# First expert matrix: transfers with 32 or 128 partitions outermost in place of 4

## The chip, the cores and the metric

The kernel runs on one NeuronCore of a Trainium2 chip. The metric is device time in microseconds (us), from start to end of one execution; less is better. Engines are called by the profile's names: PE (TensorE matmul), PEld (its weight loads), ACT (ScalarE), DVE (VectorE), POOL (GpSimd), SP (SyncE, whose queue issues most DMA transfers).

## The reference

Two layers follow each other.

1. A spectral layer on x (8 batches, 2496 positions, 256 channels, float32): a real FFT along the positions, a complex 256x256 matrix with bias per frequency, a soft threshold, and the inverse FFT.
2. A mixture of experts on its 19968 tokens: a 256x8 gate picks one of 8 experts per token (argmax), and the token gets `gate * (relu(x @ w1[e]) @ w2[e])` with w1[e] of 256x1024 and w2[e] of 1024x256, all float32.

```python
for e in range(E):
    xe = x[expert_idx == e]
    h = np.maximum(xe @ w1[e], 0.0)
    out[mask] = gate_w[mask, None] * (h @ w2[e])
```

## The kernel before

**The spectral part** (about the first 640 us) computes the FFTs as matrix products, gates each token, and writes every token's row with an indirect DMA into a DRAM buffer, `xs_dram`, in which the rows of one expert stand together. It is not touched.

**The expert part** works on tiles of 256 tokens. All tokens of a tile have the same expert, and tiles stand in the order of the experts. There are 85 tiles at most; tiles 0 to 81 always run, the last 3 sit behind branches (L902 to L909). A small table, built on the chip (`table`, L619), gives for each tile its expert (word 0), whether it needs its weights loaded (word 1: 1 for the first tile of a table and for a tile whose expert differs from the tile's before, else 0) and its first row (word 2). There are two tables: one for the first `EARLY = 5` tiles, which are made of the first seven batches while the last batch is still being finished, and one for all the others. So tile 5, the first of the second table, always loads its weights, and after it each change from one expert to the next does.

**One tile** (`step`, L864) is `up` and then `down`.

- `up` (L806): 48 matmuls of L820 make the 1024 hidden rows from the token columns (`xh`, `xl`) and w1; ACT (L825) and DVE (L826) split each result into a high and a low part. Every float32 product is made of three products of such parts.
- `down` (L831): 48 matmuls of L851 with w2 make the output; ACT scales it (L856), and POOL writes the rows to their tokens with an indirect DMA (L857).
- Inside `down`, the weights of the next tile are split: `split2` (w2: ACT L777, DVE L778) during the first half and `split1` (w1: ACT L762, DVE L763) during the second. Both are done for every tile, whether the weights are new or not. The source is the raw matrix in SBUF: `r1[0]` and `r1[1]` for w1, 128 partitions of 1024 numbers each (512 KB), and `r2[0]`, `r2[1]` for w2. There is one copy of each.
- `split1` goes through four pieces: first half of `r1[0]`, first half of `r1[1]`, then the second halves. When it is through, `weights(t + 1, 1)` (L737) issues the loads for the tile after, on SP: L716 reads the two words of the table, and L750 issues one transfer for `r1[0]` and one for `r1[1]`. Where word 1 is 0, the transfer is issued and skipped (`cond=ch`). `split2` does the same for w2.
- `load(t + 4)` (L718) stands on SP ahead of each `step` and fetches the token rows of the tile four ahead: four transfers of 64 KB (`xq`, L731), each to 32 partitions of one tile, and a small one (`xr`, L734).

SP issues in program order, so per tile its queue holds: four `xq`, one `xr`, two w2 transfers, two w1 transfers. ACT's and DVE's order is the program's order too in this part of the kernel.

**The layout of w1.** For the early tiles the token columns are transposed by PE, and partition r of `r1[q]` holds row q*128 + r of w1: source order "(c p i)" with c=2, i=32. For the later tiles DVE transposes 32x32 blocks (L794), and the partition p*32 + i of `r1[q]` holds row p*64 + q*32 + i: source order "(p c i)". Here the source of one transfer is four blocks of 32 rows, with a gap of 32 rows between them, so its outermost dimension has 4 entries, while the destination has 128 partitions.

Of the kernel before, what the change touches and what calls it, by code (L numbers as in the profile page):

```python
# [99 lines left out]
class Kernel:  # L100
# [636 lines left out]
    def weights(self, t, which):  # L737
        if t >= self.nt:
            return
        nc = self.nc  # L740
        e = self.word(0, t, E - 1)
        ch = self.word(1, t, 1)
        for q in range(2):
            if which == 1:
                order = "o (c p i) f -> c p i (o f)" if t < self.early else "o (p c i) f -> c p i (o f)"
                dst, src = self.r1[q], self.w1[bass.ds(e, 1)].rearrange(order, c=2, i=32)[q]
            else:
                src = self.w2[bass.ds(e, 1), q * 512:(q + 1) * 512, :]
                dst, src = self.r2[q], src.rearrange("o (c p) f -> p (o c) f", p=128)
            nc.sync.dma_start(dst, src, cond=ch, bounds_check="skip_entire_dma")  # L750

    def split1(self, t):
        if t >= self.nt:
# [180 lines left out]
```

## Time and profile before

| | |
|---|---|
| median of 3 runs | 1672.28 us (1671.54 to 1674.44) |
| the profiled execution, its own time | 1677.6 us |
| span of its trace, first to last instruction | 1675.8 us |
| mean granted PE clock in it | 0.965 |
| PE busy | 1563.8 us, 93% |
| DVE, ACT, POOL busy | 1240.7, 1123.4, 360.1 us |

A row of the timeline gives the start and the length in us, the engine, the line of the kernel, the operation with its tiles (out<-in), and in brackets how long the engine stood idle ahead of it and what ended that. A row of waits gives who waited for what: us in total, times, the longest. A granted clock of 1.00 is PE's full speed, 0.50 its lower level. DMA share is the mean busy share of the core's 16 DMA engines.

### The profile page before, as it was taken

To read this page: it belongs to the slowest core of one execution; us is meant where nothing else is said; L and a number is where in the kernel's file an instruction comes from. 1 tells how busy PE (TensorE), PEld (TensorE's weight loads), DVE (VectorE), ACT (ScalarE), POOL (GpSimd) and SP (SyncE) were. 2 spreads that over 40 slices of the span, in tenths; PEclk is the share of its full clock that TensorE was granted. 3 is DMA by queue.
4 is the path that set the end of the run, shared out by engine and by line. 5 is a ranking of instruction groups with operands and counts; after the bars stand their busy time and mean duration, and the time that the engine had idled before them with its cause. 6 is when DMAs were issued, how large, how long until landed. Compare 5 with 4: busy or idle time off the path is not lost. (4 is left out here: it accounts for less than half of the span.)

```text
span 1675.8 us, 37064 instructions
## 1 busy us (share of the span) xinstructions
PE 1563.8 (93%) x12334; PEld 1515.0 (90%) x12334; DVE 1240.7 (74%) x2687; ACT 1123.4 (67%) x2336; POOL 360.1 (21%) x370
## 2 busy tenths in 40 slices
PE   5899999999999989888998999999998999998997
PEld 1798999999999989878998998998998998998997
DVE  2587888888888888656876776776776776776776
ACT  2677778787877767455765675665765775675665
POOL 3002231514223243411111111111111111111111
PEclk7799999999999999989999999999999999999999
DMA  8654453636444131423123213223123123222210
GB/s 267 181 139 123 131 166 87 192 102 201 125 142 137 57 117 56 118 56 88 42 49 86 50 45 87 49 47 87 43 52 85 43 47 86 52 62 65 49 46 18
DMA packets 182080, 153.94 MB, mean 92 GB/s; under 512 B 119530, under 2 KB 153232, under 8 KB 181629
## 3 DMA queue, kind: packets, MB, share of 16 engines
q1 hardware_dynamic: 161869, 107.17, 24.4%
q0 software_dynamic: 20016, 44.36, 8.3%
q8 instruction: 100, 1.64, 0.4%
q14 instruction: 95, 0.78, 0.2%
HBM read 243.40 MB, written 66.37 MB: 185 GB/s over the span
## 5 line engine op out<-in xcount | busy, mean ns | idle before, releaser
L820 PE MATMUL ph<-xh,h 128*128 128x256 f32 x1312 | 382.4, 291 | 44.9 <-ACT h L762 43.5
L820 PE MATMUL ph<-xh,l 128*128 128x256 f32 x1312 | 381.6, 291 | 2.1 <-DVE l L763 0.6
L826 DVE SCALAR_TENSOR_TENSOR hl<-ph,hh 128x512 fp32r<-128x512 f32 x328 | 226.8, 692 | 208.2 <-ACT hh L825 198.7
L820 PE MATMUL ph<-xl,h 128*128 128x256 f32 x1312 | 379.2, 289 | 0.0
L851 PE MATMUL po<-h,hh 128*128 128x256 f32 x1312 | 371.3, 283 | 0.0
L851 PE MATMUL po<-h,hl 128*128 128x256 f32 x1312 | 371.3, 283 | 0.0
L851 PE MATMUL po<-l,hh 128*128 128x256 f32 x1312 | 371.3, 283 | 0.0
L825 ACT ACTIVATE hh<-ph 128x512 fp32r<-128x512 f32 x328 | 196.1, 598 | 252.5 <-PE ph L820 252.1
L857 POOL DMA_INDIRECT out<-o,row x154 | 155.2, 1008 | 787.0 <-ACT o L856 654.4
L820 PEld LDWEIGHTS ph<-xh,h 128*128 128x128 f32 x1312 | 260.7, 199 | 48.2 <-ACT h L762 45.6
L605 POOL DMA_INDIRECT xs_dram<-yb,pos x176 | 181.3, 1030 | 450.0 <-ACT sh L332 230.9
L820 PEld LDWEIGHTS ph<-xh,l 128*128 128x128 f32 x1312 | 260.4, 198 | 5.9 <-DVE l L763 5.9
L820 PEld LDWEIGHTS ph<-xl,h 128*128 128x128 f32 x1312 | 260.3, 198 | 0.2 <-DVE xl L803 0.2
L763 DVE TENSOR_TENSOR l<-r,h 128x512 fp32r<-128x512 f32 x332 | 209.0, 687 | 62.2 <-ACT h L762 55.6
L851 PEld LDWEIGHTS po<-h,hh 128*128 128x128 f32 x1312 | 251.9, 192 | 0.0
L851 PEld LDWEIGHTS po<-h,hl 128*128 128x128 f32 x1312 | 251.9, 192 | 0.0
L851 PEld LDWEIGHTS po<-l,hh 128*128 128x128 f32 x1312 | 251.9, 192 | 0.0
L762 ACT CAST h<-r 128x512 fp32r<-128x512 f32 x332 | 182.1, 620 | 53.3 <-DMA r<-moe_w 53.3
L778 DVE TENSOR_TENSOR l<-r,h 128x512 fp32r<-128x512 f32 x332 | 208.0, 686 | 5.6 <-ACT h L777 5.6
L777 ACT CAST h<-r 128x512 fp32r<-128x512 f32 x332 | 181.4, 620 | 10.1 <-DMA r<-moe_w 5.5
L368 DVE SCALAR_TENSOR_TENSOR y<-v,r 64x256 f32<-64x256 f32 x320 | 134.5, 420 | 36.1 <-ACT r L363 31.1
L363 ACT ACTIVATE r<-v,nlam 128x512 f32<-128x512 f32 x80 | 58.0, 725 | 86.9 <-DVE v L356 86.8
(198 smaller groups left out, 2957.6 us busy)
## 6 DMA issues: line engine op xcount, KB each, us to landing
r<-moe_w SPq DMA_DIRECT2D x336, 512.0 KB
spec_dram<-ae SPq DMA_DIRECT2D x88, 240.0 KB
t<-spec_dram SPq DMA_DIRECT2D x160, 128.0 KB
xq<-xs_dram SPq DMA_DIRECT2D x312, 64.0 KB
x<-x SPq DMA_DIRECT2D x40, 384.0 KB
x<-x SPq DMA_DIRECT2D x40, 84.0 KB
xs_dram<-yb,pos POOLq DMA_INDIRECT x176
out<-o,row POOLq DMA_INDIRECT x154
```

The lines of the kernel that those rows point to most:

```text
L363: nc.scalar.activation(r, u, AF.Relu, bias=self.nlam)
L368: nc.vector.scalar_tensor_tensor(out=y[q * 64:q * 64 + 64, kp, :], in0=u[h, q, :], scalar=LAM, in1=r[h, q, :], op0=ALU.add, op1=ALU.min)
L605: i = nc.gpsimd.indirect_dma_start(out=self.xs[:, :], out_offset=bass.IndirectOffsetOnAxis(ap=pos[:n, g:g + 1], axis=0), in_=y[:n, g, 0:XW ...
L762: nc.scalar.copy(hi[:, c, s], v)
L763: nc.vector.tensor_sub(lo[:, c, s], v, hi[:, c, s])
L777: nc.scalar.copy(hi[:, s, :], v)
L778: nc.vector.tensor_sub(lo[:, s, :], v, hi[:, s, :])
L820: nc.tensor.matmul(p[:, i, :], a[:, c, f * 128:(f + 1) * 128], v[:, c, :], start=m == 0, stop=m == 5)
L825: nc.scalar.activation(hh[:, s, :], p, AF.Relu)
L826: nc.vector.scalar_tensor_tensor(out=hl[:, s, :], in0=p, scalar=0.0, in1=hh[:, s, :], op0=ALU.max, op1=ALU.subtract)
L851: nc.tensor.matmul(p[:, :D], a[:, f, h * 128:(h + 1) * 128], v[:, f, :], start=m == 0, stop=m == 23)
L857: i = nc.gpsimd.indirect_dma_start(out=self.out[:, :], out_offset=bass.IndirectOffsetOnAxis(ap=at[h], axis=0), in_=o[:, h, :], in_offset=N ...
```

## The change

For the later tiles (t >= 5), each half of w1 is loaded by four transfers, each of 32 rows to 32 partitions (128 KB), so per tile SP issues eight w1 transfers in place of two. For the early tiles there are still two, written as 128 plain rows each. The w2 transfers stay as they are; so do the condition, the bytes, the destination's layout and the order of the program.

```diff
         for q in range(2):
-            if which == 1:
-                order = "o (c p i) f -> c p i (o f)" if t < self.early else "o (p c i) f -> c p i (o f)"
-                dst, src = self.r1[q], self.w1[bass.ds(e, 1)].rearrange(order, c=2, i=32)[q]
+            if which == 1 and t < self.early:
+                parts = [(self.r1[q], self.w1[bass.ds(e, 1), q * 128:(q + 1) * 128, :].rearrange("o p f -> p (o f)"))]
+            elif which == 1:
+                parts = [(self.r1[q][p * 32:p * 32 + 32],
+                          self.w1[bass.ds(e, 1), p * 64 + q * 32:p * 64 + q * 32 + 32, :].rearrange("o i f -> i (o f)"))
+                         for p in range(4)]
             else:
                 src = self.w2[bass.ds(e, 1), q * 512:(q + 1) * 512, :]
-                dst, src = self.r2[q], src.rearrange("o (c p) f -> p (o c) f", p=128)
-            nc.sync.dma_start(dst, src, cond=ch, bounds_check="skip_entire_dma")
+                parts = [(self.r2[q], src.rearrange("o (c p) f -> p (o c) f", p=128))]
+            for dst, src in parts:
+                nc.sync.dma_start(dst, src, cond=ch, bounds_check="skip_entire_dma")
```

## Rows read from the trace of the kernel before

**Rows 1.** Busy time of the engines, share of the span and number of instructions.

```profile
PE 1563.8 (93%) x12334; PEld 1515.0 (90%) x12334; DVE 1240.7 (74%) x2687; ACT 1123.4 (67%) x2336; POOL 360.1 (21%) x370
```

**Rows 2.** Waits from 736 us to the end (tiles 6 to 81): who waited for whom, us in total, times, longest.

```profile
ACT h L762 <- DMA r<-moe_w: 42.4, 14, 5.4
...
PE ph L820 <- ACT h L762: 29.8, 8, 4.8
```

**Rows 3.** Timeline of PE: the last matmul of tile 4; the first matmuls of tiles 6, 59 and 60; the last matmul of tile 81.

```profile
706.20 0.28 PE L851 MATMUL po<-l,hh 128*128 128x256 f32 x1
...
735.95 0.28 PE L820 MATMUL ph<-xh,h 128*128 128x256 f32 x1
...
1384.13 0.28 PE L820 MATMUL ph<-xh,h 128*128 128x256 f32 x1
...
1395.65 0.28 PE L820 MATMUL ph<-xh,h 128*128 128x256 f32 x1
...
1664.55 0.28 PE L851 MATMUL po<-l,hh 128*128 128x256 f32 x1
```

**Rows 4.** Stretches: start:end and length in us, busy us (instructions) of PE, PEld, DVE, ACT and POOL, granted clock, DMA share, GB/s. The first is ten tiles of one expert (11 to 20), then tile 60, then two parts of tile 61, the first tile of another expert.

```profile
790.69:905.89 115.20, 115.20 (x963) 115.20 (x961) 88.10 (x149) 78.86 (x147) 20.04 (x20) 1.00 0.25 61
...
1395.65:1407.17 11.52, 11.52 (x98) 11.52 (x97) 7.72 (x14) 6.58 (x12) 2.01 (x2) 1.00 0.52 158
...
1407.17:1411.90 4.73, 0.79 (x5) 0.38 (x3) 0.27 (x1) 0.63 (x2) 0.00 (x0) 0.85 0.26 78
1411.90:1417.60 5.70, 5.52 (x25) 5.23 (x26) 3.20 (x5) 2.26 (x5) 1.09 (x1) 0.52 0.29 63
```

**Rows 5.** Stretches in the same columns: while the very first w1 load (tile 0) moves; while the w1 load of tile 61 moves; while four `xq` transfers move.

```profile
622.00:624.00 2.00, 2.00 (x18) 2.00 (x18) 1.32 (x3) 1.74 (x5) 0.00 (x0) 1.00 1.01 397
...
1406.20:1410.00 3.80, 1.76 (x13) 1.35 (x11) 0.69 (x1) 0.51 (x1) 0.07 (x1) 1.00 0.31 107
1416.00:1418.00 2.00, 2.00 (x14) 2.00 (x13) 0.75 (x3) 0.66 (x2) 0.00 (x0) 0.66 0.67 124
```

**Rows 6.** Timeline of SP's issues: the weights of tile 0 (two w1 transfers, then two of w2); the two w1 transfers of tile 5; the two of tile 61; two w2 transfers in a row that are skipped; two `xq` transfers in a row; the last four weight transfers of the program.

```profile
620.29 3.65 SPq L750 DMA_DIRECT2D r<-moe_w  x4
...
705.27 0.71 SPq L750 DMA_DIRECT2D r<-moe_w  x1
...
706.35 0.56 SPq L750 DMA_DIRECT2D r<-moe_w  x1
...
1395.91 0.65 SPq L750 DMA_DIRECT2D r<-moe_w  x1
...
1396.93 0.56 SPq L750 DMA_DIRECT2D r<-moe_w  x1
...
1409.21 0.09 SPq L750 DMA_DIRECT2D r<-moe_w  x1
...
1409.65 0.08 SPq L750 DMA_DIRECT2D r<-moe_w  x1
...
1414.78 0.33 SPq L731 DMA_DIRECT2D xq<-xs_dram  x1
...
1415.32 0.32 SPq L731 DMA_DIRECT2D xq<-xs_dram  x1
...
1661.74 3.92 SPq L750 DMA_DIRECT2D r<-moe_w  x4
```

**Rows 7.** Timeline of ACT: the first piece of tile 0's w1; the split of w1 for tile 60 and the scaling after it; the scaling ahead of tile 61's w1 and the pieces of that w1.

```profile
624.37 0.62 ACT L762 CAST h<-r 128x512 fp32r<-128x512 f32 x1
...
1393.35 2.17 ACT L762 CAST h<-r 128x512 fp32r<-128x512 f32 x4
1395.86 0.47 ACT L856 ACTIVATE o<-po,xr 128x256 f32<-128x256 f32 x1 [0.34 <-PE po L851]
...
1404.50 0.48 ACT L856 ACTIVATE o<-po,xr 128x256 f32<-128x256 f32 x1 [0.22 <-PE po L851]
1406.09 0.62 ACT L762 CAST h<-r 128x512 fp32r<-128x512 f32 x1 [1.12 <-DMA r<-moe_w]
1411.27 1.66 ACT L762 CAST h<-r 128x512 fp32r<-128x512 f32 x3 [4.55 <-DMA r<-moe_w]
```

**Rows 8.** Timeline of ACT ahead of tile 5: pieces of w2, the scaling, pieces of w1.

```profile
706.42 1.14 ACT L777 CAST h<-r 128x512 fp32r<-128x512 f32 x2 [5.06 <-DMA r<-moe_w]
...
709.07 0.47 ACT L856 ACTIVATE o<-po,xw 128x256 f32<-128x256 f32 x1
715.58 0.62 ACT L762 CAST h<-r 128x512 fp32r<-128x512 f32 x1 [6.05 <-DMA r<-moe_w]
721.05 1.66 ACT L762 CAST h<-r 128x512 fp32r<-128x512 f32 x3 [4.85 <-DMA r<-moe_w]
```

**Rows 9.** SP's own waits in seven tiles without a change of expert (1180.93 to 1261.57): us in total, times, longest.

```profile
SPq L750 <- DVE l L778: 23.0, 14, 2.8
SPq L750 <- DVE l L763: 2.7, 7, 0.4
```

**Rows 10.** SP's instructions of L750 from 736 us on: number, ns of the shortest, the median and the longest, first and last start.

```profile
L750 SPq DMA_DIRECT2D r<-moe_w x306: 73/123/653, 736.2 to 1665.5; - x153
...
L750 SPq EVENT_SEMAPHORE  x305: 17/17/28, 736.6 to 1665.3; - x153
```

## The prediction, on record before the changed kernel was timed

> **What bounds the kernel now.** I read the busy shares first: PE works 93% of the span [rows 1], so time can only be won where PE stands still or runs slowly. The table of waits says where that is in tiles 6 to 81: PE waits 29.8 us for L762, the split of w1, eight times, and L762 itself waits 42.4 us for the transfers into `r1` [rows 2]. The timeline and the stretches show the rest. A tile of an undisturbed expert takes 11.52 us (1384.13 to 1395.65 [rows 3]), all of it PE, at clock 1.00, ten tiles in a row [rows 4]: there nothing but PE counts. Tile 61, the first of a new expert, waits; then the granted clock is 0.52 for 5.70 us [rows 4] after PE stood idle, so a stall is paid twice.
>
> Why L762 waits is a matter of the DMA engines. While the w1 load of tile 61 moves, their share is 0.31 at 107 GB/s; while tile 0's moved it was 1.01 at 397 GB/s [rows 5]. Both are the same megabyte in rows of 4 KB. A quarter of sixteen engines is 0.25, which four blocks as the outermost dimension explain; tile 0's source is four adjoining blocks, in effect 128 rows, and takes them all. So the late loads run on about four engines. Issued at 1395.91 and 1396.93 [rows 6], they hold ACT until 1406.09 and 1411.27 [rows 7].
>
> **The sum of what there is to win.** Tiles 6 to 81 run from 735.95 to the last matmul at 1664.55 [rows 3], 928.6 us. 76 tiles at 11.52 less the 0.1 of the last matmul make 875.4. The excess is 53.2 us: 29.8 of stalls and 23.4 of slow clock, spread over the seven changes of expert, 7.6 each. Tile 5 comes on top: from the last matmul of tile 4 at 706.20 to 735.95 [rows 3] is 29.75, against 11.64 undisturbed: 18.1 us. Together 71.3.
>
> **The change at the seven later changes of expert.** The four quarters of a half have 32 rows each, and I take them to use all engines: the `xq` transfers, which also go to 32 partitions each, reach a share of 0.67 [rows 5], which four engines can't. The price of issuing a quarter that moves isn't in the trace. From below the nearest row is `xq`, 0.54 from start to start; from above the present w1 transfers, 1.02 and 1.08 [rows 6], which are four times as big. I take 0.7, nearer to `xq` for its 32 partitions. The first quarter can start at 1395.91 as now, the eighth then at 1395.9 + 7 x 0.7 = 1400.8. Landing: tile 0's first half was issued at 620.29 and ACT had used it from 624.37 on [rows 6, 7], so at most 4.1 us for 512 KB; from below, 0.3 us of moving (128 KB at 397 GB/s [rows 5]). I take 2.2, the middle. The last byte is there at 1403.0. ACT is free for it at 1404.50 + 0.48 = 1404.98 [rows 7]. PE wants tile 61 at 1407.17. Stall and slow clock both go: 53.2 us. Cover left: 2 us on ACT, 4 on PE.
>
> **The change at tile 5.** Here the load itself is late, since SP issues it at 705.27 [rows 6], 0.9 us before PE is done with tile 4. Quarters at 0.7: the fourth starts at 707.4 and lands at 709.6; ACT ends its scaling at 709.07 + 0.47 = 709.54 [rows 8]; so the first piece is cast by 710.2 in place of 716.2. The eighth starts at 710.2, lands at 712.4, is cast by 713.0 in place of 721.7. PE thus resumes for good 8.6 us earlier; the slow clock after the stall (3.3 us a change: 23.4 over seven) stays. Saved: 8.6 of 18.1. Bounds: at worst quarters at 1.08 that land after 4.1, 1.08 x 7 + 4.1 + 0.6 = 12.3 after 705.3, so 717.5 and 4.2 saved. At best (0.54, 0.3) ACT sets the end, with the second piece cast 0.5 after the first, at 710.7: 11.0 saved, and 14.3 if the clock holds.
>
> **What it adds on SP.** Six transfers more per tile, skipped in most tiles. Two skipped ones start 0.44 apart (1409.21, 1409.65 [rows 6]), so 6 x 0.45 = 2.7 us per tile. SP waits 25.7 us in seven tiles [rows 9], 3.67 per tile: this is the cover, and 1.0 is left. Behind the new transfers stand `xq` and `xr`, read four tiles (46 us) later, and the w2 transfers of the next tile, whose wait for L778 just gets shorter. In a tile whose load moves, the six cost 6 x 0.7 = 4.2; SP falls behind by a little and catches up. The edit for early tiles costs and gains nothing: tile 0's load already has all engines [rows 5]. At the end SP's last transfer moves from 1665.7 to 1668.3 [rows 6], with the span ending at 1675.8.
>
> **What it adds on ACT and DVE.** A piece of `r1` now waits for four transfers, so six waits more per tile; a wait that is met takes SP 17 ns [rows 10], so 0.1 us. ACT has 0.34 of idle time behind L762 in each tile [rows 7], which hides it. Without that cover it would be 0.1 x 77 = 8 us.
>
> **A rule against the change.** The rows just used say that one queue's transfers overlap: `xq`s are issued 0.54 us apart and their bytes move together [rows 5, 6]. The Trainium skill (DMA: Bandwidth & Descriptors, Rules for kernel authors) advises one 128-partition transfer over two to disjoint partition halves, because they serialize on the same engines. Its section on the SWDGE path fits 2.0 us plus the bytes at 436 GB/s per transfer; by it a quarter is 2.3 us (an estimate), eight in series 18.4, and the kernel some 25 us slower than now. No run so far shows a queue of this kind in series.
>
> **Forecast.** 53.2 + 8.6 = 61.8 us less. The profiled execution took 1677.6, so 1615.8 of its kind; the median of the runs is 5.3 lower, 1672.28 - 61.8 = **1610.5**.
>
> **Rivals.**
> - *Late quarters* (0.07): each costs 1.02 and the longer landing holds: 1403.0 + 4.1 + 0.6 = 1407.7, half a microsecond after PE wanted it, and a short stall slows the clock all the same. Then the seven changes save only their 7.6 - 3.8 each, tile 5 some 4: 1672.3 - 26.6 - 4.2 = 1641.5. Against it: the bounds must hold together.
> - *Nothing changes* (0.04): a quarter still runs on four engines. The loads end as now: 1672 within 3. Against it the share of 0.67.
> - *SP becomes the bound* (0.03), the slower case: place, its queue in every tile. It decides where a skipped quarter costs more than 3.67 / 6 = 0.61; at 0.74 the gain of 61.8 is used up (6 x 0.13 x 77 tiles); at 0.8 it is 6 x 0.19 x 77 = 88, so 1699. For it: L750 has transfers of up to 653 ns [rows 10]. Against it: those move bytes; the two skipped ones take 80 to 90 ns.
> - *Quarters in series* (0.02), also slower: it decides at 15.4 / 8 = 1.9 us each, since the present pair takes 1395.91 to 1411.27. With 3.1 each (4.1 less the moving of 384 KB, 1.0), eight take 24.8: 9.4 more at eight loads, 1747. This is how the rule above would come out here, with prices from rows; against it, the overlap that they show.
>
> **How the numbers follow.** The forecast has 0.84, and its own range is 1604.8 (tile 5 saves 14.3) to 1623 (tile 5 saves 4.2, and 8 for the uncovered waits on ACT). I widen it by 3 us, what runs differ by, and towards the late quarters: 1602 to 1633. A measurement here tells 0.2%, 3.3 us, from nothing. Faster: 0.84 + 0.07 = 0.91; same: 0.04; slower: 0.05.
>
> **What would show it.** Right: no wait of PE for L762 after about 725 us; tiles at 11.52 through the changes; granted clock 1.00 from there to the end; DMA share near 1 for some 3 us at each change in place of 0.31 for 13; SP's waits in seven tiles down from 25.7 to about 7; one shorter stall, of some 6 us in all, ahead of tile 5. Wrong: SP without waits and tiles longer than 11.52 (SP bound); eight landings 2 us or more apart (series); DMA share still 0.3 (four engines). What would upset the sum most is a clock that falls for another reason once PE never rests.

## The result, and the profile after

The changed kernel takes **1611.37 us** (median of 4 runs, 1610.25 to 1615.83). The kernel before, run beside it, took 1673.36 (median of 4), so the ratio is 0.9635 [0.9622, 0.9648], 62.0 us less. The forecast was 1610.5 in 1602 to 1633.

Line numbers have moved by four: L750 is now L754 (weight transfers), L762 is L766 (split of w1), L777 and L778 are L781 and L782 (split of w2), L820 and L851 are L824 and L855 (matmuls up and down), L856 is L860 (scaling).

The busy shares of the profiled execution come first. The number of matmuls is that of [rows 1]; PE has lost 25.6 us of busy time. Of these 21.7 lie in tiles 6 to 81, where matmuls no longer run at the lower clock (stretches below), and 3.5 ahead of the expert part, which the change does not touch.

```profile
PE 1538.2 (96%) x12334; PEld 1495.3 (93%) x12334; DVE 1240.0 (77%) x2687; ACT 1123.0 (70%) x2336; POOL 358.9 (22%) x370
```

Waits of the whole run: who waited for whom, us in total, times, longest. From tile 6 on (718 us to the end) the table has no wait of PE for L766 and none of L766 for a transfer: the 29.8 and 42.4 us of [rows 2] are gone whole. What is left, 5.8 us in two waits, stands at tile 5.

```profile
PE ph L824 <- ACT h L766: 5.8, 2, 5.2
```

Timeline of PE (start, length in us, idle time before and its cause in brackets): the first matmul of tile 0, the last of tile 4, the two of tile 5 that waited, the first of tiles 6 and 61, the last of tile 81.

```profile
637.12 0.28 PE L824 MATMUL ph<-xh,h 128*128 128x256 f32 x1
...
701.92 0.28 PE L855 MATMUL po<-l,hh 128*128 128x256 f32 x1
...
707.41 0.58 PE L824 MATMUL ph<-xh,h 128*128 128x256 f32 x1 [5.21 <-ACT h L766]
...
709.49 0.58 PE L824 MATMUL ph<-xh,h 128*128 128x256 f32 x1 [0.56 <-ACT h L766]
...
723.23 0.28 PE L824 MATMUL ph<-xh,h 128*128 128x256 f32 x1
...
1356.83 0.28 PE L824 MATMUL ph<-xh,h 128*128 128x256 f32 x1
...
1598.63 0.28 PE L855 MATMUL po<-l,hh 128*128 128x256 f32 x1
```

From 723.23 to 1598.63 are 875.40 us, where [rows 3] had 928.6. The stretches say the same with the clock beside it (start:end and length, busy us and instructions of PE, PEld, DVE, ACT, POOL, granted clock, DMA share, GB/s): tiles 6 to 81; five us in which the w1 quarters of tile 61 move; tile 61 itself, the first of a new expert; the standstill ahead of tile 5.

```profile
723.30:1598.70 875.40, 875.40 (x7297) 875.40 (x7296) 680.64 (x1141) 610.31 (x1140) 152.32 (x152) 1.00 0.25 62
1347.00:1352.00 5.00, 5.00 (x44) 5.00 (x43) 3.39 (x6) 3.03 (x6) 0.24 (x1) 1.00 0.94 269
1356.83:1368.35 11.52, 11.52 (x99) 11.52 (x97) 8.96 (x16) 8.03 (x15) 2.00 (x2) 1.00 0.19 45
702.10:708.00 5.90, 0.68 (x2) 0.29 (x1) 3.20 (x5) 3.27 (x6) 1.01 (x1) 0.69 0.96 236
```

PE is busy for every one of the 875.40 us, at clock 1.00. The same tiles before, in the same columns:

```profile
735.95:1664.85 928.90, 897.33 (x7298) 892.24 (x7296) 681.65 (x1142) 610.60 (x1140) 153.16 (x152) 0.97 0.23 58
```

Tile 61 takes 11.52 us, as each of the ten tiles of one expert in [rows 4] does (by the starts in the trace they are tiles 10 to 19). The DMA share is 0.94 where [rows 5] had 0.31.

Timeline of SP: the whole group of weight transfers of tile 61, eight of w1 among them, then the first, second and eighth w1 quarter by themselves, and two skipped quarters in a row of a later tile.

```profile
1342.38 7.92 SPq L754 DMA_DIRECT2D r<-moe_w  x10
...
1345.57 0.35 SPq L754 DMA_DIRECT2D r<-moe_w  x1
...
1346.22 0.34 SPq L754 DMA_DIRECT2D r<-moe_w  x1
...
1349.98 0.32 SPq L754 DMA_DIRECT2D r<-moe_w  x1
...
1358.11 0.07 SPq L754 DMA_DIRECT2D r<-moe_w  x1
...
1358.48 0.07 SPq L754 DMA_DIRECT2D r<-moe_w  x1
```

The eight quarters go out in (1349.98 - 1345.57) / 7 = 0.63 us steps, the skipped ones in 0.37.

Timeline of ACT at the same place. All four pieces of tile 61's w1 are cast in one go at 1354.52, right behind the scaling and with no wait, 2.31 us before PE needs the first. In [rows 7] the two halves held ACT for 1.12 and 4.55 us.

```profile
1354.15 0.48 ACT L860 ACTIVATE o<-po,xr 128x256 f32<-128x256 f32 x1 [0.22 <-PE po L855]
1354.52 2.17 ACT L766 CAST h<-r 128x512 fp32r<-128x512 f32 x4
1357.03 0.47 ACT L860 ACTIVATE o<-po,xr 128x256 f32<-128x256 f32 x1 [0.34 <-PE po L855]
```

SP's own waits in seven tiles without a change of expert (1130.5 to 1211.14): 10.7 us, where [rows 9] had 25.7. SP's slack is down from 3.67 to 1.53 us a tile.

```profile
SPq L754 <- DVE l L782: 7.9, 12, 0.8
SPq L754 <- DVE l L767: 2.8, 7, 0.4
```

Ahead of tile 5, ACT still waits; SP issues the first quarter at 701.01 and the last at 705.43.

```profile
702.24 1.14 ACT L781 CAST h<-r 128x512 fp32r<-128x512 f32 x2 [5.17 <-DMA r<-moe_w]
...
705.27 0.47 ACT L860 ACTIVATE o<-po,xw 128x256 f32<-128x256 f32 x1
706.74 0.62 ACT L766 CAST h<-r 128x512 fp32r<-128x512 f32 x1 [1.00 <-DMA r<-moe_w]
708.82 1.66 ACT L766 CAST h<-r 128x512 fp32r<-128x512 f32 x3 [1.46 <-DMA r<-moe_w]
```

The tile's excess over 11.52 is 723.23 - 701.92 - 11.64 = 9.67 us, from 18.1.

The two profiled executions differ by 1677.6 - 1611.7 = 65.9: 53.2 in tiles 6 to 81, 8.4 at tile 5, and 4.3 ahead of the expert part, where tile 0 starts at 637.12 in place of 641.40. The change does not touch that part, and the medians differ by 62.0, so I count the 4.3 as a difference between executions.

### The profile page after: what moved, and what is told of

Same layout as the page of the kernel before. It is cut to its first block, busy times and chain, and to the rows that moved or that the text cites. A ratio compares the mean times of both kernels' runs of the same rounds, so it can differ in the third digit from the quotient of the medians.

```text
span 1609.9 us, 38804 instructions
## 1 busy us (share of the span) xinstructions
PE 1538.2 (96%) x12334; PEld 1495.3 (93%) x12334; DVE 1240.0 (77%) x2687; ACT 1123.0 (70%) x2336; POOL 358.9 (22%) x370
## 5 line engine op out<-in xcount | busy, mean ns | idle before, releaser
L824 PE MATMUL ph<-xh,h 128*128 128x256 f32 x1312 | 374.0, 285 | 7.2 <-ACT h L766 5.8
L824 PE MATMUL ph<-xh,l 128*128 128x256 f32 x1312 | 373.0, 284 | 0.3
L824 PE MATMUL ph<-xl,h 128*128 128x256 f32 x1312 | 372.7, 284 | 0.0
L855 PE MATMUL po<-h,hh 128*128 128x256 f32 x1312 | 371.7, 283 | 0.0
L855 PE MATMUL po<-h,hl 128*128 128x256 f32 x1312 | 371.7, 283 | 0.0
L855 PE MATMUL po<-l,hh 128*128 128x256 f32 x1312 | 371.7, 283 | 0.0
L824 PEld LDWEIGHTS ph<-xh,h 128*128 128x128 f32 x1312 | 253.1, 193 | 8.8 <-ACT h L766 6.3
L824 PEld LDWEIGHTS ph<-xh,l 128*128 128x128 f32 x1312 | 253.1, 193 | 0.9 <-DVE l L767 0.9
L824 PEld LDWEIGHTS ph<-xl,h 128*128 128x128 f32 x1312 | 253.1, 193 | 0.2 <-DVE xl L807 0.2
L855 PEld LDWEIGHTS po<-h,hh 128*128 128x128 f32 x1312 | 252.2, 192 | 0.0
L855 PEld LDWEIGHTS po<-h,hl 128*128 128x128 f32 x1312 | 252.2, 192 | 0.0
L855 PEld LDWEIGHTS po<-l,hh 128*128 128x128 f32 x1312 | 252.2, 192 | 0.0
L782 DVE TENSOR_TENSOR l<-r,h 128x512 fp32r<-128x512 f32 x332 | 208.0, 685 | 6.1 <-ACT h L781 6.1
L781 ACT CAST h<-r 128x512 fp32r<-128x512 f32 x332 | 181.5, 620 | 10.6 <-DMA r<-moe_w 6.0
L766 ACT CAST h<-r 128x512 fp32r<-128x512 f32 x332 | 181.4, 619 | 2.5 <-DMA r<-moe_w 2.5
```

What stands on the lines that cost most here:

```text
L766: nc.scalar.copy(hi[:, c, s], v)
L781: nc.scalar.copy(hi[:, s, :], v)
L782: nc.vector.tensor_sub(lo[:, s, :], v, hi[:, s, :])
L824: nc.tensor.matmul(p[:, i, :], a[:, c, f * 128:(f + 1) * 128], v[:, c, :], start=m == 0, stop=m == 5)
L855: nc.tensor.matmul(p[:, :D], a[:, f, h * 128:(h + 1) * 128], v[:, f, :], start=m == 0, stop=m == 23)
```

## The experiments

They ran on three chips: 2, 3, 4 and 8 on one, 6 and 7 on a second, 1, 5 and 9 on a third. On all three the part ahead of tile 0 takes 120 to 130 us longer than in the traces above, and tiles 0 to 4 take 74 to 80 us in place of 64.8; from tile 6 on they take the same (tiles 6 to 81 of the load of before: 929.1 in experiment 2, 928.6 above). So each is compared with runs of the kernel before on its own chip, and what counts is the difference in us. Diffs are against the changed kernel, but 5 is shown against 4 and 7 against 6. In 3, 4 and 6 only the new lines are shown; they stand in place of the three lines that experiment 2 takes out. Line numbers shift with each edit: the split of w1 is L764 in 2, L765 in 3 and L766 in 1, 4, 5, 8 and 9; the weight transfers are L758 in 6 and 7.

**1. The changed kernel again**, on the third of these chips.

> The changed kernel itself, on the chip of the other experiments if it is the same one, as their base. Theory: the gain sits in the expert part and is the same there, some 62 us: ratio to the kernel before about 0.9657 where the latter takes 1805 us, 0.963 where it takes 1672.

Measured: 1740.68 against 1800.71, ratio 0.9677 [0.9656, 0.9697], 60.0 us less. Tiles 6 to 81 take 875.4 here too. Tile 5's excess is 2.6, where loads as slow as the old one have 13.6 (experiment 2, another chip) and 13.7 (experiment 5, this chip). So the seven changes of expert are worth the same, and tile 5 is not: some 11 us here, 8.4 there. In this run SP issues tile 5's first quarter 6.1 us before the last matmul of tile 4 starts (831.72 and 837.85), in the trace above 0.9 before (701.01 and 701.92).

**2. Only the edit for the early tiles**; the later ones load as before.

```diff
-                parts = [(self.r1[q][p * 32:p * 32 + 32],
-                          self.w1[bass.ds(e, 1), p * 64 + q * 32:p * 64 + q * 32 + 32, :].rearrange("o i f -> i (o f)"))
-                         for p in range(4)]
+                parts = [(self.r1[q], self.w1[bass.ds(e, 1)].rearrange("o (p c i) f -> c p i (o f)", c=2, i=32)[q])]
```

> Only the edit for the early tiles (128 plain rows); the late tiles load as before the change. Theory: nothing, since tile 0's load already used all engines: 1672 within 3 us. Rival (the early tiles, or the start of the expert part, had a share in the gain): 1660 or less.

Measured: 1804.14 against 1804.76, ratio 1.0002 [0.9987, 1.0017]. The stalls are those of before; waits from tile 6 to the end:

```profile
PE ph L822 <- ACT h L764: 30.0, 9, 4.6
```

The early edit gives nothing and costs nothing. The whole gain is in the split of the late loads.

**3. Two transfers of 64 partitions in each half**, two blocks outermost: half as many engines as before, if the number of blocks is what sets them.

```diff
+                src = self.w1[bass.ds(e, 1)].rearrange("o (p c i) f -> c p i (o f)", c=2, i=32)[q]
+                parts = [(self.r1[q][h * 64:h * 64 + 64], src[h * 2:h * 2 + 2]) for h in range(2)]
```

> Two transfers per half of w1, each of 64 partitions, with two blocks of 32 rows outermost. Theory (the outermost dimension sets the number of engines): two engines, 128 rows of 4 KB each at 160 ns = 20.5 us for 1 MB in place of 10.2; eight loads each some 10 us later: about 1755 us (1735 to 1775), DMA share about 0.13 during the load. If the slow clock after a stall costs the same however long the stall is, the stalls alone grow. Rival (transfers half as big land earlier): between 1611 and 1672.

Measured: 1876.27 against 1804.76, ratio 1.0388 [1.0361, 1.0415], **71.5 us slower than before**, inside the 63 to 103 more that were expected. Waits from tile 6 on:

```profile
ACT h L765 <- DMA r<-moe_w: 107.7, 14, 10.2
...
PE ph L823 <- ACT h L765: 90.4, 14, 9.6
```

Splitting a load into more transfers is no gain as such: here there are twice as many as before and the load is slower, as the number of blocks says. With two blocks PE waits 90.4 us for the split, with four 30, with 32 rows outermost 0. While this load moves and hardly anything else, the share is 0.13, as expected (columns as above; over the 12 us from 1588 on, with token rows moving too, it is 0.21):

```profile
1588.00:1591.00 3.00, 0.32 (x3) 0.11 (x1) 0.00 (x0) 0.00 (x0) 0.00 (x0) 1.00 0.13 52
```

The Trainium skill (DMA: Bandwidth & Descriptors, Why a DMA increments its semaphore by 16 and not by 1) states that a transfer runs on the largest number of engines up to 16 that divides its outermost dimension on both sides. The shares agree with it: 0.13 with two blocks, 0.31 with four [rows 5], 0.94 with 32 rows.

**4. All 128 partitions in each transfer, four transfers of 256 columns**, with the four blocks outermost as before. Four engines each, but as many transfers as in the changed kernel.

```diff
+                src = self.w1[bass.ds(e, 1)].rearrange("o (p c i) f -> c p i (o f)", c=2, i=32)[q]
+                parts = [(self.r1[q][:, j * 256:j * 256 + 256], src[:, :, j * 256:j * 256 + 256])
+                         for j in range(4)]
```

> As the changed kernel, eight w1 transfers of 128 KB per tile, but each is 256 columns of all 128 partitions, so that four blocks are outermost again. Theory (the number of DMA engines decides): four engines again, now with rows of 1 KB, 256 per engine at about 49 ns (the duration of a w2 row) = 12.5 us for 1 MB in place of 10 to 11, so a load lands some 2 us later than before the change: about 1685 us (1672 to 1700), DMA share 0.25 to 0.3 during the load, PE waiting 5 to 6 us at each change of expert. Rival (smaller and more transfers decide, whatever the engines): about 1611.

Measured: 1773.68 against 1804.76, ratio 0.9832 [0.9804, 0.986], 31 us less: what neither theory had. While these loads move, the DMA share is still about a quarter (stretch of 6 us at a change of expert, columns as above), so the engines are about four, as the theory has it, and the load is no faster: from SP's first w1 issue to the last wait of the split are 15.8 us (1498.59 to 1514.36), before 15.4 (1395.91 to 1411.27). But ACT starts on the first columns before the others are there: with column pieces the split's own pieces wait only for the part that they read.

```profile
1502.00:1508.00 6.00, 6.00 (x53) 6.00 (x52) 5.01 (x9) 4.66 (x10) 0.03 (x1) 1.00 0.26 91
```

```profile
1507.59 0.61 ACT L766 CAST h<-r 128x512 fp32r<-128x512 f32 x1
1511.32 1.14 ACT L766 CAST h<-r 128x512 fp32r<-128x512 f32 x2 [3.12 <-DMA r<-moe_w]
1514.36 0.62 ACT L766 CAST h<-r 128x512 fp32r<-128x512 f32 x1 [1.89 <-DMA r<-moe_w]
```

Waits from tile 6 on: the stalls are cut from 30 to 12.7 us, the longest from 4.6 to 2.5.

```profile
PE ph L824 <- ACT h L766: 12.7, 7, 2.5
```

**5. The same with the columns in reverse order**, which takes the early start away and leaves transfers, engines and bytes as in experiment 4.

```diff
-                         for j in range(4)]
+                         for j in range(3, -1, -1)]
```

> The transfers of 256 columns again, but issued from the last columns to the first. Theory (the columns won 31 us because a piece of the split starts when its own columns have landed, while the whole load takes as long as before): now the piece that is needed first lands last, the gain goes, and it takes as long as the kernel before or up to 20 us more (ratio 1.000 to 1.012). Rival (smaller transfers land sooner in themselves): the gain stays, ratio about 0.983.

Measured: 1804.17 against 1800.71, ratio 1.0022 [1.0008, 1.0036]. The gain is gone (if anything it is 0.2% slower than before). ACT now waits for the last column piece and then casts three pieces in one go:

```profile
1537.17 1.66 ACT L766 CAST h<-r 128x512 fp32r<-128x512 f32 x3 [5.48 <-DMA r<-moe_w]
```

The first w1 issue is at 1521.31, so the load takes 15.9 us, as long as in experiment 4.

So the 31 us of experiment 4 came from the order in which columns landed, not from the number of transfers. The changed kernel's pieces hold all columns of 32 partitions, and each piece of the split needs all four: it can have nothing of this second effect, and its gain is that of the engines alone.

**6. Eight transfers of 16 rows in each half**: eight more per tile than in the changed kernel, 8 x 0.37 = 3.0 us where they are skipped, against 1.53 of slack.

```diff
+                n = (16, 16, 16, 16) if q == 0 else (16, 16, 16, 16)
+                parts = []
+                for p in range(4):
+                    for lo in range(0, 32, n[p]):
+                        parts.append((self.r1[q][p * 32 + lo:p * 32 + lo + n[p]],
+                                      self.w1[bass.ds(e, 1), p * 64 + q * 32 + lo:p * 64 + q * 32 + lo + n[p], :]
+                                      .rearrange("o i f -> i (o f)")))
```

> Each half of w1 in eight transfers of 16 rows to 16 partitions: sixteen per tile in place of eight. Theory (SP's own time per tile is the limit of such splitting): a skipped transfer costs SP 0.37 us in the changed kernel, eight more 2.96, and SP waits only 10.7 us in seven tiles there, 1.53 per tile; so SP needs 1.43 us more than the 11.52 of a tile and becomes the bound: tiles of about 12.95 us, 1611 + 76 x 1.43 = 1720 us (1700 to 1730), SP hardly waiting for DVE, PE waiting for the token tiles or the split weights. Rival (skipped transfers cost nothing that matters, the queue is far ahead): 1609 to 1615.

Measured: 1897.75 against 1813.02, ratio 1.0465 [1.0447, 1.0484], 84.7 us slower than before. The changed kernel did not run on this chip; if it wins 60 us here too (experiment 1), this is some 145 slower, and tiles 6 to 81 take 142.8 us longer than its 875.4. SP has no wait left in the six tiles from 958 to 1036.9. Its timeline, two tiles in a row:

```profile
1003.13 8.16 SPq L758 DMA_DIRECT2D r<-moe_w  x18
1012.10 1.87 SPq L731 DMA_DIRECT2D xq<-xs_dram  x4
1014.15 0.39 SPq L734 DMA_DIRECT2D xr<-xs_dram  x1
1016.08 8.14 SPq L758 DMA_DIRECT2D r<-moe_w  x18
```

From one tile's weights to the next are 12.95 us, where PE needs 11.52: SP sets the pace, though not a byte of w1 moves in these tiles. The expectation missed in size: it had 109 us more than the changed kernel, 119 at most. In the first two or three tiles after each change PE still runs at 11.52, which is quicker than expected; but the tile of each change takes 18.1 to 19.3 us and the one ahead of it 14.2 to 16.5. I put that down to the transfers that move, which come late too; no run separates it.

**7. The same for one half only**, twelve w1 transfers per tile: 4 x 0.37 = 1.5 us more, just the slack that is left.

```diff
-                n = (16, 16, 16, 16) if q == 0 else (16, 16, 16, 16)
+                n = (16, 16, 16, 16) if q == 0 else (32, 32, 32, 32)
```

> The first half of w1 in eight transfers of 16 rows, the second in four of 32: twelve per tile in place of eight. Theory: four more skipped ones are 1.48 us, just under the 1.53 that SP has free per tile: 1610 to 1618, with SP's waits near zero. Rival (cost grows with every transfer): about half of what sixteen cost, 1660.

Measured: 1778.25 against 1813.02, ratio 0.9815 [0.9798, 0.9831], 34.8 us less than before, but tiles 6 to 81 take 25.9 us longer than in the changed kernel, where at most 7 was expected. Tiles between changes do keep 11.52, but SP's slack is used up (waits in eight tiles, 1056 to 1148):

```profile
SPq L758 <- DVE hl L834: 0.3, 1, 0.3
```

So SP goes into each change of expert with no slack. The tiles there take 12.4 to 16.5 us, which I put down to the transfers that move, 0.6 us each: they put SP behind. A queue with no slack left cost time here before it was the bound of the plain tile.

**8. Tile 5's weights ahead of the token rows of tiles 6 and 7** on SP.

```diff
-        for t in range(self.early or 4, t0 + 4):
+        for t in range(self.early or 4, t0 + (3 if self.early else 4)):
...
-            if t + 4 <= main:
+            if t + 4 <= main and not (self.early and t == t0):
                 self.load(t + 4)
             self.step(t)
+            if self.early and t == t0:
+                self.load(t + 3)
+                self.load(t + 4)
```

> The changed kernel, with the token loads of tiles 6 and 7 moved on SP behind the weight loads of tile 5 (one step later). Theory (the stall left at tile 5 is SP's order: the weights stand behind two tiles' token loads, 6.5 us): the w1 load starts some 6 us earlier, PE's wait for L766 (5.8 us) and the slow clock after it (3.9) go: about 1602 us (1600 to 1606). Rival (tile 5's weights are held by the table or by r1 and r2 still in use): 1609 to 1612.

Measured: 1742.71 against 1804.76, ratio 0.9649 [0.9628, 0.9671]; the changed kernel, on another chip (experiment 1), has 0.9677 [0.9656, 0.9697]. No gain that can be told. Tile 5 does start without a wait, but three tiles' token rows now stand in a row on SP ahead of the weights of tile 6. These are skipped, yet ACT waits until their turn has come, so the wait comes back there (timelines of ACT and of PE):

```profile
853.03 1.66 ACT L766 CAST h<-r 128x512 fp32r<-128x512 f32 x3 [1.08 <-DMA r<-moe_w]
```

```profile
853.71 0.39 PE L824 MATMUL ph<-xh,h 128*128 128x256 f32 x1 [0.47 <-ACT h L766]
```

Tile 6 takes 12.97 us. Most of the stall was moved, not removed: tiles 6 to 81 have 1.8 us of excess in place of 0, tile 5 has 0. And there was little to win, if tile 5's excess is on this chip what it is in experiment 1, 2.6; I had worked with 9.7.

**9. Token rows read three tiles ahead in place of four, behind the weights**, in every tile.

```diff
-        for t in range(self.early or 4, t0 + 4):
+        for t in range(self.early or 4, t0 + 3):
             self.load(t)
         for t in range(t0, main):
-            if t + 4 <= main:
-                self.load(t + 4)
             self.step(t)
+            if t + 3 <= main:
+                self.load(t + 3)
```

> The changed kernel with the token rows of a tile loaded three tiles ahead, behind the weights, in place of four tiles ahead, in front of them: ahead of tile 5's weights SP issues one tile's token loads, not three, and none piles up behind. Theory (what is left at tile 5 is SP's order, and the 1.45 us lost at tile 6 in the last version came from three tiles' token loads in a row): tile 5 starts without a wait of more than 0.5 us, no later tile is longer than 11.6, and the kernel is 5 to 10 us below the changed one. Rival (a lead of three tiles is too short, or the table is what holds tile 5): the same as the changed one or slower.

Measured: 1735.66, ratio 0.9640 [0.9623, 0.9656], 5.0 us below the changed kernel beside it (1740.68). This is the best version. PE's timeline from the first matmul of tile 4 to the last of tile 81:

```profile
825.97 0.28 PE L824 MATMUL ph<-xh,h 128*128 128x256 f32 x1
...
1724.41 0.28 PE L855 MATMUL po<-l,hh 128*128 128x256 f32 x1
```

That is 898.44 us, 78 tiles at 11.52 less 0.12: every tile from 4 on is undisturbed, tile 5 too. The two profiled executions differ by 3.0, of which tile 5's excess is 2.6. The rest of the 5.0 stays open; the part ahead of the experts varies by as much between executions (4.3 in the traces above).

## Why the prediction was right

**The sum to win at the seven changes** (53.2) came out to a tenth: 928.6 - 875.40. It held because it was read as a difference of two stretches of one trace. Of its two terms, the stalls could be named in the table of waits and the slow clock could not. The 23.4 was what the stalls left over; by PE's busy time (897.33 before, 875.68 after, with the last matmul) the clock made 21.7 of it, and short waits the rest. After the change the clock is 1.00 throughout, so the second did hang on the first.

**Why the load was slow** was the step on which all stood, and it rested on one row for each case: 0.31 with four blocks, 1.01 with 128 rows. Experiment 3 bears it out from the other side (0.13 with two blocks), experiment 2 shows that nothing else in the change matters, and 4 and 5 show that four engines keep the load as slow as before (15.8 and 15.9 us) though as many transfers carry it as in the changed kernel. "Nothing changes" is out.

**Issue and landing of a quarter.** I took 0.7 and 2.2; the issue is 0.63. The last quarter of tile 5 goes out at 705.43 and ACT's wait for it ends at 708.82, so it landed after 3.4: longer than taken, inside the bounds 0.3 to 4.1. I wrote "DMA share near 1 for some 3 us", which took tile 0's 397 GB/s at share 1.01 [rows 5] to hold for quarters too. It does not. At the change of tile 61 the share is 0.94 for five us, at 269 GB/s; and at tile 5, in a stretch in which only w1 rows move:

```profile
704.00:707.00 3.00, 0.00 (x0) 0.00 (x0) 1.48 (x3) 1.78 (x4) 0.99 (x1) 0.55 0.93 216
```

So all engines are at work, but a row of 4 KB takes longer: 0.27 us on average in these three, by the transfer records of the trace, against 0.16 while tile 0's w1 moved. The rate is twice that of four engines (107 GB/s), not four times. A quarter goes to 32 partitions, a half of tile 0's load to 128; whether that is why was not tried. At the seven changes the error cost nothing: ACT was ready for the last piece at 1354.52 with the bytes there, so the cover of 2 us on ACT was enough.

**Tile 5**: 9.5 forecast to remain, 9.67 measured. That these agree to 0.2 is luck, since errors of both signs lie in it: quarters 0.07 faster each, 0.5 us over seven, against a landing 1.2 longer. Together they put the matmul behind the second piece at 709.49, 7.6 after the last matmul of tile 4, where I had 6.8; what follows it costs 2.1, where the old trace gave 2.6 (18.1 less the 15.5 to 721.7). The 2.6 of experiment 1 shows how little of this term is the kernel's own: SP was further ahead there. The saving was some 11 us there, my best case without the clock (11.0).

**SP's queue**: 0.45 was taken for a skipped quarter; 0.37 was seen in one pair, and (25.7 - 10.7) / 7 / 6 = 0.36 by the slack used. So SP waits 10.7 us in seven tiles and not about 7. "SP becomes the bound" was a real mechanism, only not at this size: experiment 6 is that rival at work. With six transfers more it decides from 0.61 for a skipped one; with the fourteen more of experiment 6, from 3.67 / 14 = 0.26.

**Late quarters** did not come: no wait of PE for L766 after tile 5. **Quarters in series** is out: in tile 5 eight quarters were issued within 4.4 us and all were used by 708.82, 7.8 after the first, where in series at the price I gave eight would take 24.8. The Trainium skill's rule (DMA: Bandwidth & Descriptors, Rules for kernel authors) that two transfers to disjoint partition halves serialize does not decide here. It speaks of halves that use all engines anyway, and the transfer replaced here had about four; by the measurement the change pays.

**What it adds on ACT and DVE** was costed at nothing behind 0.34 us of idle time, and nothing is to be seen: the scaling of tile 61 still has 0.34 idle before it at 1357.03.

## What to carry to other kernels

When a load is late, read the DMA share while it moves. Here 0.13 and 0.31 went with two and four blocks outermost: the shape of the transfer, not the bandwidth, set its time, and cutting it so that the outermost dimension is long won the stalls and the slow clock after them. Read the GB/s beside the share: a share near 1 moved 397 GB/s in one shape and 216 in another. Before adding transfers to a queue, count its own waits per tile and price a skipped transfer like any other instruction; stop before the slack is gone: with none left, the tiles in which bytes do move took 12.4 to 16.5 us (experiment 7). If the consumer works in pieces, let each transfer carry what one piece reads: with a slow load that alone brought half of the gain (experiment 4).

## What I had not expected of the hardware

- **Stalls three times as long brought hardly more slow clock.** PE's busy time in tiles 6 to 81 beyond the 875.7 of the changed kernel is the cost of the lower clock. Before the change it is 21.7 us, 3.1 a change, with stalls of 4.3 a change. In experiment 3 it is 24.5, 3.5 a change, with stalls of 12.9. In experiment 4 it is 8.5, 1.2 a change, with stalls of 1.8. So a stall that is only shortened still pays part of the price.
- **A DMA share near 1 is not yet the full rate.** The 32-row quarters keep the engines 93% busy and move 216 GB/s, where tile 0's load moves 397 at 1.01 (tile 5's load in the trace of experiment 1 is as slow, 0.28 us a row); the cause stays open.
- **A skipped transfer costs SP over half of one that moves**: 0.37 us from start to start against 0.63.
- **One kernel's first part took 120 to 130 us longer on other chips**, with tiles 6 to 81 equal to 0.5 us in 929. Between 100 and 600 us PE is busy for 85 to 87 us of each 100 in the trace of experiment 2, at granted clocks of 0.90 to 0.93; in the trace of the kernel before it is 95 to 98 at 0.97 to 1.00. Why was not tried. It means that a difference in us could be carried from one chip to another here, a ratio less well.
